# One table for the order of the attention steps in a fused attention and two-MLP kernel

## The chip, the cores and the metric

The kernel runs on one core of a Trainium2 chip. The metric is device time in microseconds (us), the median of three runs. Five engines work side by side, each on its own queue of instructions, strictly in order: TensorE (PE: matrix products; PEld is its weight load), VectorE (DVE), ScalarE (ACT), GpSimd (POOL) and SyncE (SP, which here only issues transfers). Engines wait for each other by semaphores. An instruction that waits holds up everything behind it on its own engine.

## The reference

Causal attention over 2 batches of 12 heads, 448 positions and head width 64, followed by two MLPs on the 896 resulting rows of 768 values (all in float32):

```python
scores = scale * np.matmul(q, k.transpose(0, 1, 3, 2))
scores = np.where(mask, -1000000000.0, scores)      # mask: strictly above the diagonal
scores = scores - np.max(scores, axis=-1, keepdims=True)
attn = np.exp(scores)
attn = attn / (np.sum(attn, axis=-1, keepdims=True) + 1e-09)
x = np.matmul(attn, v)                               # heads side by side: 896 x 768
h = np.maximum(x @ w_in, 0.0);   x = h * h @ w_out   # first MLP, width 2048
h = x @ w_in2;  g = h / (1 + exp(-1.702 h));  out = g @ w_out2
```

## The kernel before

Heads are taken two at a time: a *pair* p (12 in all) is two heads on the two halves of the 128 partitions. Queries are cut in blocks of 128 rows; the scores of a pair come in groups. Group 0 holds query blocks 2 and 0 of both heads (two PSUM banks), group 1 holds block 1 of both heads (two banks), and group 2 the last 64 queries of both heads in one bank. The first pair has group 0 cut in two (groups 3 and 4).

A pair goes through these steps. **Scores** (`scores`, PE). **Minima** (`shifted`, DVE, L266): one instruction per block adds the mask, scales by -1/8, writes the block to SBUF (`pnh`, `pnl`) and returns the row minimum into `stat`; each is followed by a short read of the accumulator. **Exponentials** (`exponentials`, ACT, L283), in place, which also return the row sums. **Sums and reciprocals** (`normalise`, L293 and L294: add 1e-9, then the reciprocal, both on DVE). **Scaling** by the reciprocal (L296, POOL). **Transposes** (`transpose`, PE, L311): 32 blocks into four banks, two banks (one per half) for `g` = 0 and two for `g` = 1. **Copies** out of these banks to `pt` (`keep_transposed`, L316): of each couple of banks one on ACT and one on DVE. **Values** (`values`, PE, L335) into one bank, then the rounded copy (`keep_values`, ACT, L347) and the remainder (`keep_rest`, a subtraction on DVE, L351).

The schedule is written by hand: what stands first in the program stands first in each engine's queue. Ahead of the loop there is a prologue with pairs 0 and 1 up to their exponentials. The loop then makes 12 *turns*; turn p does scores, minima, exponentials and the scaling of group 0 for pair p+2, scaling of the other groups for pair p+1, transposes and copies for pair p, and values for pair p-1. In turns 3 to 8 it also takes pieces of the decoding of the first two weight chunks (64-bit integers into two float parts, `split_w_steps`, on ACT and DVE, L100 to L108), and in turns 10 and 11 pieces of two more. In turns 10 and 11, which have no new scores, PE gets products of the first MLP (`filler`) between the other steps.

PSUM has eight banks from one pool (`ps_p`), and a step that needs a bank waits until the bank's last user has read it. A turn takes ten banks. In the turns between, values (`x`) of a turn take the bank in which the first scores of group 0 of the same turn lay, so they wait for the minima of that head.

Behind the attention the MLPs follow, one product after the other on PE, with weight decoding on DVE and ACT beside them. The change does not touch them.

Of the kernel before, what the change touches and what calls it, by code (L numbers as in the profile page):

```python
# [14 lines left out]
ALU = mybir.AluOpType  # L15
# [3 lines left out]
B, H, S, D = 2, 12, 448, 64  # L19
# [16 lines left out]
WARM = 7  # L36


@with_exitstack
def attention_mlps_kernel(  # L40
# [11 lines left out]
    nc = tc.nc  # L52
# [63 lines left out]
    X = {}  # L116
# [21 lines left out]
    with tc.tile_pool(name="const", bufs=1) as cp, tc.tile_pool(  # L138
# [119 lines left out]
        def shifted(p, g):  # L258
# [4 lines left out]
            work.sort(key=lambda u: u[0])  # L263
# [23 lines left out]
        def normalise(p, gs, eng=nc.gpsimd):  # L287
            if p >= n:
                return
            st = stat[p]  # L290
            work = [u for g in gs for k in range(1 if g == 2 else 2) for u in units(p, g, k)]
            lo, hi = min(u[3] for u in work), max(u[3] for u in work) + 1
            nc.vector.tensor_scalar(st[:, 2, lo:hi], st[:, 1, lo:hi], 1e-9, None, op0=ALU.add)  # L293
            nc.vector.reciprocal(st[:, 2, lo:hi], st[:, 2, lo:hi])  # L294
            for _, _, pn, s, _ in work:
                eng.tensor_scalar(pn, pn, st[:, 2, s : s + 1], 1.0, op0=ALU.mult, op1=ALU.mult)  # L296

        def transpose(p, g):

            if g == 0:  # L300
                PT[p] = qk_p.tile([128, 2, 1024], F32, tag="pt", name="pt")
# [12 lines left out]
        def keep_transposed(p, g):  # L314
            for k, tp in enumerate(tbank.pop((p, g))):
                (nc.vector.tensor_copy if k else nc.scalar.copy)(PT[p][:, k, 512 * g : 512 * g + 512], tp)  # L316
# [38 lines left out]
        for g in (3, 1, 4, 2):  # L355
            scores(0, g)
            shifted(0, g)
            exponentials(0, g)
            if g == 4:
                normalise(0, (3, 1))  # L360
        normalise(0, (4,))
        scores(1, 0)
        scores(1, 1)
        shifted(1, 0)
        normalise(0, (2,), nc.vector)
        exponentials(1, 0)
        scores(1, 2)
        shifted(1, 1)
        exponentials(1, 1)
        shifted(1, 2)  # L370
        exponentials(1, 2)
        normalise(1, (0,))
# [5 lines left out]
        def filler(p):  # L378
            if p + 2 >= n:
                first_term(0, *spare_terms.pop(0), X)  # L380

        def some(k):
            for _ in range(k):
                if decode:
                    decode.pop(0)()

        for p in range(n):
# [9 lines left out]
            many = 2 if p > 9 else 1  # L397
            scores(p + 2, 0)
            scores(p + 2, 1)
            shifted(p + 2, 0)  # L400
            normalise(p + 1, (1, 2))
            exponentials(p + 2, 0)
            filler(p)
            transpose(p, 0)
            transpose(p, 1)
            keep_transposed(p, 0)
            some(many)
            filler(p)
            shifted(p + 2, 1)
            exponentials(p + 2, 1)  # L410
            keep_transposed(p, 1)
            normalise(p + 2, (0,))
            some(many - 1)
            if p > 0:
                values(p - 1)
                keep_values(p - 1)
            filler(p)
            scores(p + 2, 2)
            shifted(p + 2, 2)
            exponentials(p + 2, 2)  # L420
            if p > 0:
                keep_rest(p - 1)
            some(many)
            filler(p)
            some(many - 1)
        first_term(0, 5, 0, X)
        values(n - 1)
        while decode:
            decode.pop(0)()
        keep_values(n - 1)  # L430
        keep_rest(n - 1)
# [144 lines left out]
```

## Time and profile before

| what | us |
|---|---|
| median of 3 runs (551.65 to 560.81) | 551.95 |
| the profiled execution, device time | 551.52 |
| its span in the trace | 549.7 |
| PE busy in the span | 538.6 |
| DVE busy | 354.0 |
| ACT busy | 268.0 |
| POOL busy | 69.3 |

The attention takes about the first 85 us of the span, the MLPs the rest. A view by windows gives the busy time of each engine in a stretch. A timeline gives instructions in order with the idle time of their engine ahead of them in brackets, and what ended it. A start-to-start distance in a timeline is what an instruction costs in a full queue; the duration beside it also holds the instruction's tail, which overlaps with the next one. The granted TensorE clock is 1.00 in every stretch shown.

### The profile page before, as it was taken

What the parts mean: (1) busy time and instruction counts of PE and PEld (TensorE: products, weight loads), DVE (VectorE), ACT (ScalarE), POOL (GpSimd) and SP (SyncE); (2) the same over time, 40 slices, a digit from 0 to 9 for tenths busy, and PEclk for the clock granted to TensorE, in tenths of its full rate; (3) what the DMA queues carried; (4) which work ended last, traced back from release to release, by engine and by line L of the source; (5) the groups of instructions that cost most, each with busy time, mean ns of one, the idle gap of its engine ahead of it and who ended that gap; (6) DMA issues with size and microseconds to landing.
All of it is one profiled execution on the core that took longest, in us unless ns stands there. A gap on an engine that the chain in (4) does not pass through costs nothing.

```text
span 549.7 us, 8778 instructions
## 1 busy us (share of the span) xinstructions
PE 538.6 (98%) x3199; PEld 479.4 (87%) x3199; DVE 354.0 (64%) x806; ACT 268.0 (49%) x610; POOL 69.3 (13%) x115
## 2 busy tenths in 40 slices
PE   8998899999999999999999999999999999999997
PEld 4665678999999999999999999999999999999996
DVE  6988976666666667555465467888878874544420
ACT  6988855666666564233222264555555432222210
POOL 5765630000000000000000011222221100000000
PEclk9999999999999999999999999999999999999999
DMA  7862113343334434333332234334334363443000
GB/s 219 284 188 89 32 30 95 107 116 97 105 115 125 139 129 154 122 109 110 120 86 85 59 87 116 100 103 115 113 109 143 120 199 107 140 148 116 33 35 33
DMA packets 25018, 62.30 MB, mean 113 GB/s; under 512 B 4496, under 2 KB 9744, under 8 KB 24976
## 3 DMA queue, kind: packets, MB, share of 16 engines
q1 hardware_dynamic: 24256, 61.17, 36.6%
q10 hardware_dynamic: 720, 0.57, 0.3%
q8 instruction: 25, 0.41, 0.3%
q14 instruction: 17, 0.14, 0.1%
HBM read 58.98 MB, written 2.75 MB: 112 GB/s over the span
## 4 chain that ended last, share of the span: by engine, by line
PE 89%; ACT 6%; DVE 3%; issue 1%; DVEq 0%; ACTq 0%
PE h L125 14%; PE y L127 14%; PE y L126 14%; PE h L127 14%; PE h L126 14%; PE y L125 14%; ACT pnh L283 4%; DVE pnh L266 2%; PE x L335 1%; ACT pt L316 1%; PE s L238 1%; ACT x L347 1%; PE warm L220 1%; PE s L231 1%; PE t L311 0%
## 5 line engine op out<-in xcount | busy, mean ns | idle before, releaser
L101 ACT CAST wsplit<-m 128x384 fp32r<-128x384 f32 (+1 forms) x112 | 62.7, 560 | 241.5 <-PE y L127 128.4
L125 PE MATMUL h<-x,wsplit 128*128 128x448 f32 x384 | 141.1, 367 | 0.0
L125 PE MATMUL y<-h,wsplit 128*128 128x448 f32 x384 | 140.2, 365 | 0.0
L127 PE MATMUL y<-h,wsplit 128*128 128x448 f32 x384 | 140.2, 365 | 0.0
L126 PE MATMUL y<-h,wsplit 128*128 128x448 f32 x384 | 140.2, 365 | 0.0
L126 PE MATMUL h<-x,wsplit 128*128 128x448 f32 x384 | 140.2, 365 | 0.0
L127 PE MATMUL h<-x,wsplit 128*128 128x448 f32 x384 | 140.2, 365 | 0.0
L102 DVE TENSOR_TENSOR wsplit<-m,wsplit 128x384 fp32r<-128x384 f32 (+1 forms) x112 | 68.8, 614 | 64.1 <-ACT wsplit L101 64.0
L100 DVE CUSTOM_DVE_ANT_0 m<-m,e 128x768 uint16<-128x768 uint16 (+1 forms) x112 | 78.9, 704 | 47.4 <-ACT e L105 34.1
L125 PEld LDWEIGHTS h<-x,wsplit 128*128 128x128 f32 x384 | 72.1, 188 | 6.1 <-DVE stat L293 0.2
L126 PEld LDWEIGHTS h<-x,wsplit 128*128 128x128 f32 x384 | 72.1, 188 | 5.8 <-issue 0.2
L125 PEld LDWEIGHTS y<-h,wsplit 128*128 128x128 f32 x384 | 72.1, 188 | 5.7
L127 PEld LDWEIGHTS y<-h,wsplit 128*128 128x128 f32 x384 | 72.1, 188 | 5.7
L127 PEld LDWEIGHTS h<-x,wsplit 128*128 128x128 f32 x384 | 72.1, 188 | 5.7
L126 PEld LDWEIGHTS y<-h,wsplit 128*128 128x128 f32 x384 | 72.1, 188 | 5.7
L108 DVE SCALAR_TENSOR_TENSOR m<-wraw,m 128x384 uint32<-128x384 uint32 (+1 forms) x112 | 70.3, 628 | 0.0
L105 ACT ACTIVATE e<-wraw 128x384 uint32<-128x384 uint32 (+1 forms) x112 | 67.8, 605 | 0.0
L473 POOL TENSOR_TENSOR h<-g,h 128x448 fp32r<-128x448 f32 x16 | 24.0, 1499 | 336.8 <-ACT h L468 336.8
L106 DVE TENSOR_SCALAR m<-wraw 128x384 uint32<-128x384 uint32 (+1 forms) x112 | 42.6, 380 | 0.0
L283 ACT ACTIVATE pnh<-pnh,stat 128x128 f32<-128x128 f32 (+2 forms) x72 | 35.7, 497 | 7.4 <-DVE stat L266 7.2
L296 POOL TENSOR_SCALAR pnh<-pnh,stat 128x384 f32<-128x384 f32 (+2 forms) x72 | 34.6, 500 | 28.0 <-ACT pnh L283 18.7
L468 ACT CAST h<-g 128x448 fp32r<-128x448 f32 x64 | 34.1, 568 | 3.7 <-DVE g L466 3.5
(54 smaller groups left out, 372.4 us busy)
## 6 DMA issues: line engine op xcount, KB each, us to landing
wraw<-w1i SPq DMA_DIRECT2D x32, 384.0 KB, 3.1
wraw<-w1o SPq DMA_DIRECT2D x24, 512.0 KB, 3.7
wraw<-w2i SPq DMA_DIRECT2D x32, 384.0 KB, 3.1
wraw<-w2o SPq DMA_DIRECT2D x24, 512.0 KB, 3.8
kr<-kT SPq DMA_DIRECT2D x11, 224.0 KB, 3.9
yT<-o SPq DMA_DIRECT2D x11, 224.0 KB, 2.0
v<-v SPq DMA_DIRECT2D x6, 384.0 KB, 3.9
qr<-qT SPq DMA_DIRECT2D x10, 224.0 KB, 4.1
```

The source lines that it names most:

```text
L100: tt(out=m, in0=m, in1=e, op=ALU.add)
L101: nc.scalar.copy(s[:, 0, :], w)
L102: rests.append(lambda: tt(out=s[:, 1, :], in0=w, in1=s[:, 0, :].bitcast(F32), op=ALU.subtract))
L105: lambda: nc.scalar.mul(e, lo, 2.0**-29),
L106: lambda: ts(m, hi, 3, 0x3FFFFFFF, op0=ALU.logical_shift_left, op1=ALU.bitwise_and),
L108: lambda: stt(m, in0=hi, scalar=0xC0000000, in1=m, op0=ALU.bitwise_and, op1=ALU.bitwise_or),
L125: nc.tensor.matmul(ps, ws[:, 0, w], rhs[:, 0, b, :], start=first, stop=False)
L126: nc.tensor.matmul(ps, ws[:, 0, w], rhs[:, 1, b, :], start=False, stop=False)
L127: nc.tensor.matmul(ps, ws[:, 1, w], rhs[:, 0, b, :], start=False, stop=last)
L283: nc.scalar.activation(pn, pn, ACTF.Exp, bias=st[:, 0, s : s + 1], scale=-1.0, accum_out=st[:, 1, s : s + 1])
L296: eng.tensor_scalar(pn, pn, st[:, 2, s : s + 1], 1.0, op0=ALU.mult, op1=ALU.mult)
L468: nc.scalar.copy(h[:, 0, b, :], gs[b])
```

## The change

All steps of the attention are now entries of two tables, `PROLOGUE` and `TURN`: a step's name, and for which pair it is done (in `TURN` a lag relative to the turn). One function `do` runs an entry once per pair. The steps' own arithmetic is as before. These things differ:

- In a turn, PE now does all scores of pair p+2 (groups 0, 2, 1), then both transposes of pair p, then the values of pair p-1. The scores of group 2 were last.
- The minima of groups 1 and 2 and their exponentials move one turn later (lag 1 where it was 2); those of group 0 stay at lag 2, and are last in the turn. On DVE they go head by head (`min0h`).
- The copies out of the transpose banks move one turn later (lag -1), ahead of most other work; three kinds of `kT`: `A` on ACT, `D` on DVE, `M` on ACT for even pairs and on DVE for odd ones. Before, each pair had two on ACT and two on DVE.
- The rounded copy of the values (`xc`) and the remainder (`xr`) move to the turn after the values (lag -2).
- The addition of 1e-9 (`add0`, `add12`) moves from DVE to POOL, except in the prologue; the reciprocals (`rec`) stay on DVE, apart from their sums.
- The prologue computes both pairs' scores of groups 0 and 1 ahead of group 2 and orders minima and exponentials accordingly.
- The first-MLP products in turns 10 and 11 stand together in front of the transposes. Decoding pieces are taken at two places of the turn.

The core of the diff:

```diff
+TURN = (
+    ("kT01A", -1), ("xc", -2), ("some1", 0), ("nrm0", 0), ("kT00M", -1), ("fill", 0), ("min2", 1), ("rec12", 0),
...
+    ("kT10D", -1), ("exp2", 1), ("s0", 2), ("add0", 1), ("xr", -2), ("s2", 2), ("min0h", 2), ("add12", 1),
+    ("s1", 2), ("rec0", 1), ("fill", 0), ("T0", 0), ("T1", 0), ("x", -1), ("exp0", 2),
+)
...
-            work.sort(key=lambda u: u[0])
+            if not by_head:
+                work.sort(key=lambda u: u[0])
...
-            nc.vector.tensor_scalar(st[:, 2, lo:hi], st[:, 1, lo:hi], 1e-9, None, op0=ALU.add)
-            nc.vector.reciprocal(st[:, 2, lo:hi], st[:, 2, lo:hi])
-            for _, _, pn, s, _ in work:
-                eng.tensor_scalar(pn, pn, st[:, 2, s : s + 1], 1.0, op0=ALU.mult, op1=ALU.mult)
...
+        def sums(p, gs, eng):
+            _, at = places(p, gs)
+            eng.tensor_scalar(stat[p][:, 2, at], stat[p][:, 1, at], 1e-9, None, op0=ALU.add)
...
-        def keep_transposed(p, g):
-            for k, tp in enumerate(tbank.pop((p, g))):
-                (nc.vector.tensor_copy if k else nc.scalar.copy)(PT[p][:, k, 512 * g : 512 * g + 512], tp)
+        def keep_transposed(p, g, k, eng):
+            copy = nc.scalar.copy if eng == "A" or (eng == "M" and p % 2 == 0) else nc.vector.tensor_copy
+            copy(PT[p][:, k, 512 * g : 512 * g + 512], tbank[p, g][k])
...
-            scores(p + 2, 0)
-            scores(p + 2, 1)
-            shifted(p + 2, 0)
-            normalise(p + 1, (1, 2))
-            exponentials(p + 2, 0)
-            filler(p)
-            transpose(p, 0)
-            transpose(p, 1)
-            keep_transposed(p, 0)
-            some(many)
-            filler(p)
-            shifted(p + 2, 1)
-            exponentials(p + 2, 1)
-            keep_transposed(p, 1)
-            normalise(p + 2, (0,))
-            some(many - 1)
-            if p > 0:
-                values(p - 1)
-                keep_values(p - 1)
-            filler(p)
-            scores(p + 2, 2)
-            shifted(p + 2, 2)
-            exponentials(p + 2, 2)
-            if p > 0:
-                keep_rest(p - 1)
...
+            for step, lag in TURN:
+                if step == "fill":
+                    filler(p)
+                elif step.startswith("some"):
+                    some(int(step[4:]) * (1 if p < 10 else 3))
+                elif p:
+                    do(step, p + lag)
```

How the queues moved, at three places. First DVE, where the remainder of the values meets the minima of group 0 (`x` is the remainder, `pnh` and `pnl` take the blocks, `t` are transpose banks, a row with `stat` alone reads the accumulator). Before, at the end of turn 1 and the start of turn 2:

```order
L316 COPY pt<-t 128x512
L293 TENSOR_SCALAR stat<-stat 128x4
L294 RECIPROCAL stat<-stat 128x4
L266 ISA pnl_128,stat<-s,last 128x448
L266 ISA stat 128x1
L351 TENSOR_TENSOR x<-x 128x448
L266 ISA pnh_126,stat<-s,mask 128x384
```

The change, in turn 2:

```order
L339 COPY pt<-t 128x512 x2
L374 TENSOR_TENSOR x<-x 128x448
L283 ISA pnh_126,stat<-s,mask 128x384
L283 ISA stat 128x1
L283 ISA pnh_126,stat<-s,mask 128x128
L283 ISA stat 128x1
L283 ISA pnh_126,stat<-s,mask 128x384
```

The remainder still stands right ahead of the minima of group 0, but behind two copies of an older pair; the addition is gone from this queue, and the two blocks of one head now follow each other.

Second ACT, from one rounded copy of the values (`CAST x`) to the next. Before, turns 1 to 2:

```order
L316 COPY pt<-t 128x512
L347 CAST x<-x 128x448
L283 ACTIVATE pnl_128,stat<-pnl_128,stat 128x448
L283 ACTIVATE pnh_126,stat<-pnh_126,stat 128x384 x2
L283 ACTIVATE pnh_126,stat<-pnh_126,stat 128x128 x2
L316 COPY pt<-t 128x512
L283 ACTIVATE pnh_126,stat<-pnh_126,stat 128x256 x2
```

The change, turn 2:

```order
L339 COPY pt<-t 128x512
L370 CAST x<-x 128x448
L300 ACTIVATE pnh_125,stat<-pnh_125,stat 128x256 x2
L300 ACTIVATE pnl_128,stat<-pnl_128,stat 128x448
L300 ACTIVATE pnh_126,stat<-pnh_126,stat 128x384
L300 ACTIVATE pnh_126,stat<-pnh_126,stat 128x128
L300 ACTIVATE pnh_126,stat<-pnh_126,stat 128x384
```

Between the rounded copy and the exponentials of group 0 (`pnh_126`) stood one exponential of 448; now there stand two of 256 more, all of the pair before.

Third PE, one turn. Before (`t` transposes of pair 2, `x` values of pair 1, then scores of group 2 of pair 4 and of groups 0 and 1 of pair 5):

```order
L311 MATMUL t<-ident,pnh_127 128x64 x24
L311 MATMUL t<-ident,pnl_130 128x64 x8
L335 MATMUL x<-pt,v_94 64x384 x2
L335 MATMUL x<-pt,v_94 64x64 x2
L335 MATMUL x<-pt,v_94 64x256 x2
L335 MATMUL x<-pt,v_94 64x64 x2
L335 MATMUL x<-pt,v_94 64x128 x2
L335 MATMUL x<-pt,v_94 64x64 x4
L231 MATMUL s<-kr,ql_86 128x448
L238 MATMUL s<-kr,qr 128x384 x2
L238 MATMUL s<-kr,qr 128x128 x2
L238 MATMUL s<-kr,qr 128x256 x2
```

The change (all scores of pair 4, then the same transposes and values):

```order
L254 MATMUL s<-kr,qr 128x384 x2
L254 MATMUL s<-kr,qr 128x128 x2
L247 MATMUL s<-kr,ql_86 128x448
L254 MATMUL s<-kr,qr 128x256 x2
L334 MATMUL t<-ident,pnh_127 128x64 x24
L334 MATMUL t<-ident,pnl_130 128x64 x8
L358 MATMUL x<-pt,v_94 64x384 x2
L358 MATMUL x<-pt,v_94 64x64 x2
L358 MATMUL x<-pt,v_94 64x256 x2
L358 MATMUL x<-pt,v_94 64x64 x2
L358 MATMUL x<-pt,v_94 64x128 x2
L358 MATMUL x<-pt,v_94 64x64 x4
```

PE does the same matrix work; the scores of group 2 went from behind the values to between the other scores.

## Rows read from the trace of the kernel before

**Rows 1.** The page: span, then PE's busy time, share and instructions.

```profile
span 549.7 us, 8778 instructions
PE 538.6 (98%) x3199; PEld 479.4 (87%) x3199; DVE 354.0 (64%) x806; ACT 268.0 (49%) x610; POOL 69.3 (13%) x115
```

**Rows 2.** Windows: length, busy (instructions) per engine, clock; prologue, turns 2 to 9, rest.

```profile
4.28:14.12 9.84, 8.24 (x73) 5.09 (x72) 8.28 (x44) 8.15 (x31) 4.37 (x10) 1.00 0.80 265
...
20.62:69.39 48.77, 44.30 (x597) 30.26 (x593) 43.50 (x176) 42.95 (x142) 28.41 (x57) 1.00 0.41 127
69.39:90.00 20.61, 20.61 (x208) 16.23 (x205) 13.48 (x30) 10.63 (x25) 3.75 (x8) 1.00 0.21 58
```

**Rows 3.** Windows of single turns: the two without decoding on DVE, the longest of eight.

```profile
20.62:26.40 5.78, 5.44 (x78) 3.73 (x75) 5.06 (x22) 5.21 (x19) 3.45 (x8) 1.00 0.97 308
26.40:32.06 5.66, 5.43 (x78) 3.71 (x74) 5.00 (x22) 5.21 (x18) 3.06 (x8) 1.00 0.61 184
...
56.98:63.38 6.40, 5.44 (x79) 3.72 (x75) 6.13 (x24) 5.24 (x18) 3.99 (x8) 1.00 0.20 63
```

**Rows 4.** Timeline of PE over one turn: start, duration, instruction, [idle before, releaser].

```profile
20.62 1.02 PE L231 MATMUL s<-kr,ql 128*128 128x448 f32 x2
21.57 1.57 PE L238 MATMUL s<-kr,qr 64*128 64x384 f32 x12
22.98 0.92 PE L311 MATMUL t<-ident,pnh 64*128 64x64 f32 x24
...
24.49 1.98 PE L335 MATMUL x<-pt,v 128*64 128x384 f32 x28 [0.34 <-DVE stat L266]
26.40 1.02 PE L231 MATMUL s<-kr,ql 128*128 128x448 f32 x2
```

**Rows 5.** Waits from 14 to 71 us, by engine: total, times, longest.

```profile
PE x L335 <- DVE stat L266: 4.9, 9, 1.0
...
DVE x L351 <- ACT x L347: 2.5, 6, 0.5
...
ACT pnh L283 <- DVE stat L266: 5.8, 8, 1.2
```

**Rows 6.** Timeline of all engines where turn 5 ends and turn 6 begins.

```profile
46.35 0.53 ACT L347 CAST x<-x 128x448 fp32r<-128x448 f32 x1
...
46.91 0.62 DVE L351 TENSOR_TENSOR x<-x 128x448 fp32r<-128x448 f32 x1 [0.47 <-ACT x L347]
...
48.04 0.61 ACT L283 ACTIVATE pnh<-pnh,stat 128x384 f32<-128x384 f32 x1 [0.50 <-DVE stat L266]
...
48.75 1.98 PE L335 MATMUL x<-pt,v 128*64 128x384 f32 x28 [0.39 <-DVE stat L266]
```

**Rows 7.** Timeline: an addition, a reciprocal and a copy on DVE, and what follows.

```profile
48.82 0.17 DVE L293 TENSOR_SCALAR stat<-stat 128x3 f32<-128x3 f32 x1
49.02 0.18 DVE L294 RECIPROCAL stat<-stat 128x3 f32<-128x3 f32 x1
49.11 0.66 DVE L316 COPY pt<-t 128x512 f32<-128x512 f32 x1
49.69 0.41 DVE L266 CUSTOM_DVE_ANT_0 pnh<-s,mask 128x256 f32<-128x256 f32 x1
```

**Rows 8.** Groups of POOL by form: count, total busy us, mean ns, idle before.

```profile
L296 POOL TENSOR_SCALAR pnh<-pnh,stat 128x128 f32<-128x128 f32 x24 | 9.3, 389 | 3.2 <-ACT pnh L283 3.2
...
L565 POOL MEMSET const-float32-0.0<- 128x1 f32 x1 | 0.1, 103 | 0.2 <-issue 0.2
```

**Rows 9.** Timeline: one decoding step on DVE, in turn 7 and in turn 10.

```profile
59.51 0.73 DVE L108 SCALAR_TENSOR_TENSOR m<-wraw,m 128x384 uint32<-128x384 uint32 x1
...
76.02 0.55 DVE L108 SCALAR_TENSOR_TENSOR m<-wraw,m 128x384 uint32<-128x384 uint32 x1
```

**Rows 10.** Timeline: PE and DVE where turn 1 begins.

```profile
14.12 1.02 PE L231 MATMUL s<-kr,ql 128*128 128x448 f32 x2 [0.72 <-DVE stat L266]
...
14.20 0.41 DVE L293 TENSOR_SCALAR stat<-stat 128x3 f32<-128x3 f32 x1
```

More of the change, by code (lines that the diff above doesn't have):

```diff
@@ L36 @@
 WARM = 7
+PROLOGUE = (
[4 rows of a table added]
+)
+TURN = (
[4 rows of a table added]
+)
 @with_exitstack
@@ L256, in units, with shifted @@
             ]
-        def shifted(p, g):
+        def shifted(p, g, by_head):
             if p >= n:
@@ L353, in keep_rest, with do @@
             )
[L355 to L372, printed above, removed]
+        done = set()
+        def do(step, p):
+            if not 0 <= p < n:
+                return
+            name = step.rstrip("ADMh")
+            kind, gs = name.rstrip("0123456789"), [int(g) for g in name if g.isdigit()]
+            if kind in ("add", "rec", "nrm"):
+                if any((kind, p, g) in done for g in gs):
+                    return
+                done.update((kind, p, g) for g in gs)
+            elif (name, p) in done:
+                return
+            done.add((name, p))
+            on_vector = step.endswith("D")
+            if kind == "s":
+                scores(p, gs[0])
+            elif kind == "min":
+                shifted(p, gs[0], step.endswith("h"))
+            elif kind == "exp":
+                exponentials(p, gs[0])
+            elif kind == "add":
+                sums(p, gs, nc.vector if on_vector else nc.gpsimd)
+            elif kind == "rec":
+                reciprocals(p, gs)
+            elif kind == "nrm":
+                normalise(p, gs, nc.vector if on_vector else nc.gpsimd)
+            elif kind == "T":
+                transpose(p, gs[0])
+            elif kind == "kT":
+                keep_transposed(p, *gs, step[-1])
+            else:
+                {"x": values, "xc": keep_values, "xr": keep_rest}[kind](p)
+        for step, p in PROLOGUE:
+            do(step, p)
         load_qk(3)
@@ L378, in filler @@
         def filler(p):
-            if p + 2 >= n:
+            if p + 2 >= n and spare_terms:
                 first_term(0, *spare_terms.pop(0), X)
@@ L396, in attention_mlps_kernel @@
                 decode += split_w_steps(len(wsplit)) + [lambda i=len(wsplit) + 3: load_w(i)]
[L397 to L427 removed]
+            for step, lag in TURN:
[5 more added lines that the diff above has]
+                    do(step, p + lag)
+                else:
+                    for q in range(lag + 1):
+                        if q or step.startswith(("T", "kT", "x")):
+                            do(step, q)
+        for p in (n, n + 1):
+            for step, lag in TURN:
+                if p + lag < n and not step.startswith(("some", "fill")):
+                    if p + lag == n - 1 and step == "x":
+                        while spare_terms:
+                            first_term(0, *spare_terms.pop(0), X)
+                        first_term(0, 5, 0, X)
+                    do(step, p + lag)
         while decode:
             decode.pop(0)()
[L430 to L431 removed]
     hp_ = ctx.enter_context(tc.tile_pool(name="hp_", bufs=KF))
```

15 lines of the change are left out of this document (9 added, 6 removed), and 5 rows, old and new, of tables (PROLOGUE, TURN).

## The prediction

> **What bounds the kernel now.** I read the page first: PE is busy 538.6 of 549.7 us [rows 1], so no order of the other engines can give back more than the 11.1 us in which PE stands idle, and that is 2.0% of the time. I then cut the span by windows [rows 2]. From 69.39 us on PE has no gap that matters (20.61 of 20.61 up to 90 us); the MLPs behind it are one product after another. What can be won lies in front: a prologue to 14.12, then turns 1 to 9. I count a turn from one score matmul of group 2 to the next: turn 1 begins at 14.12 [rows 10], turn 9 ends at 69.39, nine turns in 55.3 us, 6.14 each. The eight from 20.62 on take 48.77 us, 6.10 each.
>
> What does such a turn need? PE's timeline over turn 2 [rows 4] runs from 20.62 to 26.40, 5.78, with 0.34 of idle time: 5.44 us of work that no order removes. DVE is busy 43.50 us in the eight turns, 5.44 each, but unevenly [rows 2, 3]: 5.03 in the two turns without decoding, so (43.50 - 10.06) / 6 = 5.57 in the others. ACT has 42.95 / 8 = 5.37, POOL 28.41 / 8 = 3.55. Three engines thus need about 5.4 and the turn takes 6.1: the missing 0.7 are waits in a ring. The sums of waits name it [rows 5]: PE's values wait for DVE's minima (4.9 us, 9 times), ACT's exponentials for DVE's minima (5.8, 8 times), DVE's remainder for ACT's copy (2.5, 6 times). Rows 6 show it once, in order: ACT rounds the values at 46.35; DVE waits 0.47 for that and subtracts at 46.91; only then come the minima of group 0, for which ACT has waited 0.50 when it starts at 48.04, and PE 0.39 when its values start at 48.75, since they need the bank of the first head.
>
> **The ring, term by term.** In the new order DVE's remainder still stands ahead of the minima, but the rounded copy is asked of ACT at the head of the turn, while DVE's subtraction stands behind the minima of groups 2 and 1 and two copies, so that wait goes. ACT's exponentials of group 0 stand last in ACT's turn, behind 1.6 us or more of exponentials of the pair before, so that they need the minima later. PE does all scores first; the values come behind the scores that they share a bank with by 0.95 for group 2 (20.62 to 21.57 [rows 4]), some 0.5 of the 1.41 for groups 0 and 1, and 1.17 for the transposes (22.98 to 24.49 less the idle 0.34): 2.6 us, in which the minima of the second head have to come. The remainder and the minima of both heads take 1.91 together (46.91 to 48.82 [rows 6, 7]). So each of the three waits has cover. What is late next is whichever engine has most work.
>
> **Work that changes engine.** Two additions per turn leave DVE: 0.20 from an addition to the next instruction [rows 7], 0.40 in all. Half a copy per turn comes to DVE from ACT: a copy costs 0.58 there [rows 7], so 0.29. DVE has 5.03 - 0.40 + 0.29 = 4.92 without decoding and 5.57 - 0.11 = 5.46 with it. ACT loses about as much as DVE gets, an estimate, 5.37 - 0.29 = 5.08. POOL gets two tiny additions, which no row shows there. Below, a one-column memset took 0.10; above, a 128x128 scaling 0.39 [rows 8]. I take 0.3, nearer the scaling because it is the same operation. POOL then has 3.55 + 0.6 = 4.15, at most 4.33, with over a microsecond free.
>
> The change also adds waits. Both reciprocals on DVE now wait for POOL. Behind the one of group 0, DVE's last step of a turn, stand the next turn's minima of groups 2 and 1, and PE's next scores want their banks. POOL runs scaling of group 0, then of groups 1 and 2, then the two additions; from one reciprocal to the addition that the next one needs it has 3.55 + 0.3 = 3.9 us of work in a turn of 5.4, so I cost this at nothing; without that cover it would cost the overhang. On ACT the rounded copy, now second in the turn, waits for the end of PE's values, with a copy and all exponentials behind it; 5.08 us of work in a 5.44 turn leave 0.36 for that, and less in turns that also hold a decoding step and the extra copy.
>
> **Sum for the turns.** The floor is max(5.44, 4.92) = 5.44 without decoding and max(5.44, 5.46) = 5.46 with it: nine turns in 49.1. The ceiling I set by the two turns of before that have no decoding, 5.78 and 5.66 [rows 3], which still hold the ring. Engines that are 92 to 100% full and wait for each other in strict order don't reach the floor; I take 5.6, the middle: 50.4, which is 4.9 less than 55.3.
>
> **The prologue.** DVE is full there (8.28 of 9.84 busy [rows 2]), and its work stays, except that the additions for groups 1 and 2 of pair 1 and group 0 of pair 2 go to POOL: 0.44 for the one at 14.20, which waited, with its reciprocal next at 14.64 [rows 10], and 0.20 for the other. The copies of pair 0 go behind the first scores' minima into turn 1. PE's wait of 0.72 ahead of the scores of group 2 [rows 10] goes, but the second transpose bank now wants a minimum of pair 2. Bounds 0 and 0.9; I take 0.5.
>
> **The end of the attention, and the MLPs.** Behind turn 9 PE has the same transposes, values and nine products left, and had no gap [rows 2]. The new order puts four products (12 matmuls) in front of each transpose, time for the scaling and copies of the pair; I cost it at nothing. If that cover is short, PE idles there, up to about 1 us. The transfers on SP stand in the same order as before, and keep the 16 DMA engines 41% busy over the turns, so starting 5 us sooner finds them ready. Clock: granted 1.00 in every stretch before; PE gets only denser.
>
> Sum: 4.9 + 0.5 = 5.4. The profiled execution took 551.52, which gives 546.1. The median of the runs shown is 551.95, 0.43 more; on that scale I predict **546.5 us**.
>
> **A rule that speaks against it.** Row first: a decoding step on DVE took 0.73 in turn 7, beside a busy POOL, and 0.55 in turn 10 without [rows 9]. The Trainium skill, "GPSIMD Engine Reference", section 1 (Specifications), says that GpSimd shares its SBUF interfaces with VectorE and that they contend when a VectorE instruction has two SBUF inputs or runs in a two-port mode. This trace agrees with it.
>
> **Rivals.**
> - *DVE and POOL collide.* Two-input steps stretch by 0.73 / 0.55 = 1.33. Decoding is (5.57 - 5.03) x 6 = 3.2 us on DVE; POOL now works at the head of each DVE turn, where these pieces stand. If all of it stretched once more: 3.2 x 0.33 = 1.1, all on the bound: 547.6. For it: rows 9. Against: some of the decoding is stretched already in the 3.2, and minima, copies and remainders read PSUM.
> - *The ring moves instead of opening.* ACT runs late, so its rounded copy, DVE's remainder, the minima behind it and PE's values are late in turn. For it: ACT has only 0.36 to spare. Then turns stay at 5.9 to 6.1: saved 0.4 to 2.2, with the prologue 549.3 to 551.1.
> - *Slower: POOL becomes the loop.* The reciprocal of group 0 waits for POOL's addition, the next scaling for the reciprocal. That loop is 3.55 + a plus two handovers of about 0.1, so 3.75 + a with a the price of one addition. It decides from a = 1.7 on (turn 5.44), passes the time of before at a = 2.4 (turn 6.14), and slows the kernel by 2% (11 us over nine turns, turn 7.4) at a = 3.6. Against: that is nine times the dearest near row, 0.39. A turn of 6.5 would give 551.95 + 9 x 0.36 - 0.5 = 554.7.
> - *Better than forecast.* Floor turns and the full 0.9: 6.2 + 0.9 = 7.1, so 544.8. More than 2% would need nearly all of PE's 11.1 us, including the wait for the first transfers at the start.
>
> **How the numbers follow.** Forecast (turns of 5.45 to 5.85, with the prologue between its bounds 544.8 to 549.3): 0.68. Collision as the deciding effect: 0.10. Ring moved: 0.15. Loop through POOL: 0.04. Better than 544.5: 0.03. The range from 544.3 to 550.2 holds the forecast, the collision and the better half of the moved ring. Two per cent either way, about what a measurement of this kernel tells from no change, is 540.9 and 563.0: faster 0.02, within 0.94, slower 0.04.
>
> **What the profile after would show.** Turns of about 5.6 between score matmuls of group 2; waits of DVE's remainder for ACT near zero; values waiting less than 0.2 a turn for minima; DVE busy about 5.0 and 5.5 a turn; POOL's additions at 0.1 to 0.4 and no reciprocal waiting for them; PE reaching the first MLP product about 5.4 sooner and nothing changed behind. The prediction is wrong if reciprocals wait for POOL, if ACT's rounded copy waits and the minima with it, or if PE idles in turns 10 and 11.

## The result and the profile after

The changed kernel takes 546.27 us (median of 4 runs, 545.8 to 546.54); the kernel before, run beside it, takes 551.65. Several kernels, the one before among them, had single executions some 9 us longer, and the medians given from here on leave those out. The ratio is 0.990, with a 95% interval from 0.989 to 0.992: 5.4 us or about 1% less, within two per cent, 0.2 us from the forecast of 546.5 and inside its range. The profiled execution took 546.54 us, against 551.52 of before.

The page comes first: the span, PE's busy time with that of the other engines, and the shares of the chain that ended last.

```profile
span 544.6 us, 8744 instructions
PE 539.2 (99%) x3199; PEld 480.6 (88%) x3199; DVE 353.3 (65%) x791; ACT 265.7 (49%) x604; POOL 75.7 (14%) x136
PE 98%; DVE 1%; issue 0%; ACT 0%; ACTq 0%
```

Against [rows 1] the span is 5.1 us shorter, and PE's busy time is 0.6 us longer. Idle time of PE was 549.7 - 538.6 = 11.1 and is 544.6 - 539.2 = 5.4. In the kernel before, the chain that ended last had 89% on PE, 6% on ACT and 3% on DVE; now it is PE nearly throughout.

The windows answer to [rows 2] and [rows 3]. A turn is counted from one first score matmul to the next (group 0 now; group 2 before). The rows are the prologue, turn 1, turns 2 to 9 together, the first of them, and the rest to 90 us. Columns: window, length, then busy time (instructions) of PE, PEld, DVE, ACT, POOL, the granted clock, the DMA share and GB/s.

```profile
4.28:14.44 10.16, 9.38 (x75) 5.85 (x75) 8.75 (x46) 8.46 (x32) 5.56 (x12) 1.00 0.79 264
14.44:20.53 6.09, 6.09 (x75) 4.17 (x74) 6.09 (x27) 6.09 (x23) 4.00 (x11) 1.00 0.95 281
20.53:65.27 44.74, 44.74 (x596) 31.14 (x593) 42.75 (x166) 40.76 (x137) 32.40 (x73) 1.00 0.46 139
...
65.27:90.00 24.73, 24.73 (x231) 20.80 (x228) 16.56 (x34) 12.36 (x28) 6.32 (x12) 1.00 0.24 65
```

Turn 9 now ends at 65.27. In turns 2 to 9 the profile shows no idle time on PE: 44.74 of 44.74 us, where it had 44.30 of 48.77 in eight turns of before. The mean turn is 44.74 / 8 = 5.59; six of the eight are 5.56, turns 4 and 6 are 5.70 and 5.68, and turn 1, ahead of them, is 6.09. Behind, PE is still without a gap. The two kernels' turns don't start at the same matmul, so for a like count I take the start of the first scores of group 0 in turn 1 in both: 15.07 before, 14.44 after. From there to the same place nine turns later (before: 69.39 and 0.95 of group 2) it was 70.34 - 15.07 = 55.27 and is 65.27 - 14.44 = 50.83. So the turns gave 4.4 us and the prologue 0.6.

PE's busy time is modelled, and in the three longer turns it hides a wait for a PSUM bank. The scores of group 0 take 1.07 from their start to the next scores in the six short turns, but 1.22 in turn 4, 1.18 in turn 6 and 1.61 in turn 1. Turn 4 begins like this:

```profile
31.18 0.57 ACT L339 COPY pt<-t 128x512 f32<-128x512 f32 x1
31.65 1.29 PE L254 MATMUL s<-kr,qr 64*128 64x384 f32 x8
32.87 1.02 PE L247 MATMUL s<-kr,ql 128*128 128x448 f32 x2
```

ACT's copy out of a transpose bank ends at 31.18 + 0.57 = 31.75, and the second head's scores, which take that bank, load their first weights at 31.81. In turn 6 it is the same (copy until 42.41 + 0.57 = 42.98, weights at 43.03). In turn 1 the second head's weights, at 14.98, wait for a minimum on DVE. The three waits come to 0.8 us.

The waits from 13 to 66 us answer to [rows 5] (engine, tile, line, what it waited for: total, times, longest):

```profile
ACT x L370 <- PE x L358: 3.7, 6, 0.9
...
DVE x L374 <- ACT x L370: 1.1, 2, 0.8
...
PE t L334 <- DVE stat L283: 0.8, 1, 0.8
...
ACT pnh L300 <- POOL stat L311: 0.4, 1, 0.4
```

Two of the three waits of the ring are gone: PE's values no longer wait for minima (4.9 us before), nor ACT's exponentials (5.8 before). The remainder's wait for ACT fell from 2.5 to 1.1. The only wait of a PE matmul that the view lists is a single one of a transpose, 0.8, ahead of turn 1. In their place stands ACT's rounded copy, which waits for the end of PE's values; nothing late follows from it, as this timeline of all engines at the head of turn 5 shows. It answers to [rows 6] (start, duration, engine, line, instruction, [idle before, releaser]).

```profile
37.47 0.54 ACT L370 CAST x<-x 128x448 fp32r<-128x448 f32 x1 [0.62 <-PE x L358]
...
38.06 0.61 DVE L374 TENSOR_TENSOR x<-x 128x448 fp32r<-128x448 f32 x1
...
38.59 0.54 DVE L283 CUSTOM_DVE_ANT_0 pnh<-s,mask 128x384 f32<-128x384 f32 x1
38.79 0.52 ACT L300 ACTIVATE pnh<-pnh,stat 128x256 f32<-128x256 f32 x1
...
39.79 0.66 ACT L300 ACTIVATE pnl<-pnl,stat 128x448 f32<-128x448 f32 x1
...
40.44 0.61 ACT L300 ACTIVATE pnh<-pnh,stat 128x384 f32<-128x384 f32 x1
```

The rounded copy runs right behind the values. Then come the remainder and the first minima of group 0 on DVE, at 38.06 and 38.59. While DVE makes these, ACT is busy with the exponentials of groups 1 and 2 of the pair before, and those of group 0 then start at 40.44 with nothing to wait for.

### The profile page after: what moved, and what is told of

Read it like the earlier page. It is cut to its first block, busy times and chain, and to the rows that moved or that the text cites. A ratio compares the mean times of both kernels' runs of the same rounds, so it can differ in the third digit from the quotient of the medians.

```text
span 544.6 us, 8744 instructions
## 1 busy us (share of the span) xinstructions
PE 539.2 (99%) x3199; PEld 480.6 (88%) x3199; DVE 353.3 (65%) x791; ACT 265.7 (49%) x604; POOL 75.7 (14%) x136
## 4 chain that ended last, share of the span: by engine, by line
PE 98%; DVE 1%; issue 0%; ACT 0%; ACTq 0%
PE h L141 14%; PE h L143 14%; PE y L143 14%; PE y L141 14%; PE y L142 14%; PE h L142 14%; PE x L358 4%; PE s L254 3%; PE t L334 2%; PE s L247 2%; DVE pnh L283 1%; PE warm L236 1%; DVE pnl L283 0%; DVE pnl L319 0%; DVE stat L315 0%
## 5 line engine op out<-in xcount | busy, mean ns | idle before, releaser
L124 DVE SCALAR_TENSOR_TENSOR m<-wraw,m 128x384 uint32<-128x384 uint32 (+1 forms) x112 | 70.3, 628 | 0.0
L122 DVE TENSOR_SCALAR m<-wraw 128x384 uint32<-128x384 uint32 (+1 forms) x112 | 43.1, 384 | 0.0
L319 POOL TENSOR_SCALAR pnh<-pnh,stat 128x384 f32<-128x384 f32 (+2 forms) x72 | 35.7, 516 | 7.8 <-DVE stat L315 5.2
L300 ACT ACTIVATE pnh<-pnh,stat 128x384 f32<-128x384 f32 (+2 forms) x72 | 35.8, 502 | 1.9 <-DVE stat L283 1.5
```

The costliest lines, as they stand in the source:

```text
L122: lambda: ts(m, hi, 3, 0x3FFFFFFF, op0=ALU.logical_shift_left, op1=ALU.bitwise_and),
L124: lambda: stt(m, in0=hi, scalar=0xC0000000, in1=m, op0=ALU.bitwise_and, op1=ALU.bitwise_or),
L300: nc.scalar.activation(pn, pn, ACTF.Exp, bias=st[:, 0, s : s + 1], scale=-1.0, accum_out=st[:, 1, s : s + 1])
L319: eng.tensor_scalar(pn, pn, stat[p][:, 2, s : s + 1], 1.0, op0=ALU.mult, op1=ALU.mult)
```

## The experiments

The theory: the gain comes from where the rounded copy `xc` stands in ACT's queue, ahead of some 1.6 us of other exponentials, so that the remainder and the minima behind it are done when ACT and PE ask for them. The rivals: the additions on POOL, which take 0.4 us a turn off DVE; the lag of the copies; the prologue; PE's order of scores.

**1. The one move undone: the rounded copy behind the other exponentials.** Everything else is as in the changed kernel.

```diff
-    ("kT01A", -1), ("xc", -2), ("some1", 0), ("nrm0", 0), ("kT00M", -1), ("fill", 0), ("min2", 1), ("rec12", 0),
+    ("kT01A", -1), ("some1", 0), ("nrm0", 0), ("kT00M", -1), ("fill", 0), ("min2", 1), ("rec12", 0),
...
-    ("kT10D", -1), ("exp2", 1), ("s0", 2), ("add0", 1), ("xr", -2), ("s2", 2), ("min0h", 2), ("add12", 1),
+    ("kT10D", -1), ("exp2", 1), ("xc", -2), ("s0", 2), ("add0", 1), ("xr", -2), ("s2", 2), ("min0h", 2), ("add12", 1),
```

> The changed kernel with one entry moved: ACT's rounded copy of the values stands behind the exponentials of groups 1 and 2, right ahead of those of group 0, as it did before the change (there with one exponential between). Theory (the ring runs from the rounded copy over DVE's remainder and minima to ACT's exponentials of group 0, and it was opened by the 1.6 us of exponentials that now stand behind the rounded copy): ACT must idle from the copy's end to the first minimum, 0.1 + 0.54 + 0.48 + 0.1 = 1.2 a turn, and its loop becomes 1.97 + 0.47 + 0.24 + 0.3 + 0.99 + 0.65 + 0.43 + 1.2 = 6.25 instead of 5.56: nine turns cost 5 to 6 us, 551 to 552.5, all of the gain. Rival (the gain lies in the order of the scores on PE, the lag of the copies or the load of DVE): 546.3, no change.

Measured: 553.37 us, ratio to the kernel before 1.003 [1.002, 1.004]. That is 7.1 us more than the changed kernel: the whole gain and more. Its waits from 14 to 71 us:

```profile
ACT pnh L300 <- DVE stat L283: 9.8, 8, 1.3
DVE x L374 <- ACT x L370: 8.6, 7, 1.8
...
PE t L334 <- DVE stat L283: 2.7, 7, 0.4
```

And its timeline where the ring closes:

```profile
33.99 0.65 ACT L300 ACTIVATE pnl<-pnl,stat 128x448 f32<-128x448 f32 x1
...
34.64 0.51 ACT L370 CAST x<-x 128x448 fp32r<-128x448 f32 x1
35.18 0.62 DVE L374 TENSOR_TENSOR x<-x 128x448 fp32r<-128x448 f32 x1
...
35.72 0.55 DVE L283 CUSTOM_DVE_ANT_0 pnh<-s,mask 128x384 f32<-128x384 f32 x1
...
36.37 0.62 ACT L300 ACTIVATE pnh<-pnh,stat 128x384 f32<-128x384 f32 x1 [1.23 <-DVE stat L283]
```

Now all other exponentials come first, the rounded copy after them, and ACT has nothing left to do while DVE makes remainder and minima: it idles 1.23 ahead of the exponentials of group 0, at about the 1.2 expected. The ring is back, longer than in the kernel before. The mechanism held, and so did its price: the nine turns take 56.81 us (14.27 to 71.08) instead of 50.83, 6.0 more where 5 to 6 were expected. I had not counted what follows: in turns 10 and 11 another 1.1 us goes, with a transpose that waits 0.52 for POOL's scaling at 80.28.

**2. The one move alone, in the kernel before.** The rounded copy, with the values ahead of it, goes ahead of group 1's exponentials.

```diff
             transpose(p, 1)
+            if p > 0:
+                values(p - 1)
             keep_transposed(p, 0)
             some(many)
+            if p > 0:
+                keep_values(p - 1)
             filler(p)
...
             some(many - 1)
-            if p > 0:
-                values(p - 1)
-                keep_values(p - 1)
```

> The kernel before with one step moved: ACT's rounded copy of the values of pair p-1 goes ahead of the exponentials of groups 1 and 2 of its turn (the values' matmuls keep their place on PE in turns 1 to 9; in turns 10 and 11 they come ahead of one first-MLP product). Nothing else of the change: additions on DVE, old order of scores, copies and minima, old prologue. Theory (the place of that copy on ACT is the cause): the waits of DVE's remainder for ACT and of ACT's exponentials for the minima go, turns fall from 6.10 to 5.5 to 5.7, 547.0 to 548.5. Rival (several parts are needed together, a PSUM bank keeps the ring closed): 551 to 552. The additions and the prologue would then be worth the rest.

Measured: 548.07 us, ratio 0.993 [0.991, 0.996], as expected. This one move brings 3.6 of the 5.4 us. Window over its turns 2 to 9, and below it the waits from 14 to 71 us that are left of [rows 5]:

```profile
20.70:66.00 45.30, 43.45 (x596) 29.74 (x592) 42.72 (x176) 42.91 (x141) 29.05 (x57) 1.00 0.47 141
```

```profile
PE x L335 <- DVE stat L266: 2.2, 5, 0.5
ACT pnh L283 <- DVE stat L266: 1.6, 4, 0.5
```

Turns are 45.30 / 8 = 5.66, those without a stall 5.44 to 5.45, which is PE's own work. The values' wait fell from 4.9 to 2.2, the exponentials' from 5.8 to 1.6; the remainder's wait for ACT doesn't occur any more.

**3. Additions: back on DVE in the changed kernel.**

```diff
-    ("kT10D", -1), ("exp2", 1), ("s0", 2), ("add0", 1), ("xr", -2), ("s2", 2), ("min0h", 2), ("add12", 1),
+    ("kT10D", -1), ("exp2", 1), ("s0", 2), ("add0D", 1), ("xr", -2), ("s2", 2), ("min0h", 2), ("add12D", 1),
```

> The changed kernel with the additions of 1e-9 given back to DVE (all else as changed). In the changed kernel turns 2 to 9 take 5.59 us each with PE never idle, while DVE is busy 42.75 / 8 = 5.34. Theory (the ring of waits was cut, PE is the bound, DVE is next): DVE gets 0.40 a turn, 5.74 on average, so turns go to about 5.75, 1.5 us in all: 547.8. Rival (taking the additions off DVE is what carries the gain): nine turns lose 0.40 each, 3.6 us, 549.9 or more. Rival (DVE has spare time in every turn): 546.3, no change.

Measured: 546.42 us, ratio 0.991 [0.989, 0.993], which can't be told from the changed kernel; six of turns 2 to 9 are still 5.56, turns 4 and 6 5.69 and 5.66. The theory missed, the second rival (spare time on DVE) held. Window over turns 2 to 9:

```profile
20.42:65.13 44.71, 44.71 (x596) 31.08 (x592) 44.37 (x180) 40.83 (x137) 28.49 (x57) 1.00 0.47 145
```

DVE is busy 44.37 of 44.71 us, and PE still shows no gap. DVE's work just fits under PE's.

**4. Additions: on POOL in the kernel before, and on POOL beside the move of the rounded copy.** The first is the diff below; the second is it and the diff of experiment 2 together.

```diff
-        def normalise(p, gs, eng=nc.gpsimd):
+        def normalise(p, gs, eng=nc.gpsimd, adds=nc.vector):
...
-            nc.vector.tensor_scalar(st[:, 2, lo:hi], st[:, 1, lo:hi], 1e-9, None, op0=ALU.add)
+            adds.tensor_scalar(st[:, 2, lo:hi], st[:, 1, lo:hi], 1e-9, None, op0=ALU.add)
...
-            normalise(p + 1, (1, 2))
+            normalise(p + 1, (1, 2), adds=nc.gpsimd)
...
-            normalise(p + 2, (0,))
+            normalise(p + 2, (0,), adds=nc.gpsimd)
```

> The kernel before with one part of the change alone: in the turns the additions of 1e-9 go from DVE to POOL. Theory (DVE's additions are not in the ring: it runs over the remainder, the first minimum, and ACT): 551.2 to 551.8, hardly any change. Rival (the load of DVE bounds the turns of before): 0.40 a turn over nine turns, 548.1.

> The kernel before with ACT's rounded copy early (548.1 by itself) and also the additions of the turns on POOL (552.4 by itself, no gain). In the first of these, values still wait for minima 2.2 us in five turns, those with decoding on DVE. Theory (with the ring open DVE's load counts in those turns): 0.40 less on DVE takes most of these waits, 546.5 to 547.3. Rival (the remaining waits come from a decoding step between the remainder and the minima, which the additions don't touch, or reciprocals wait for POOL): 548.1 or up to 1 us more.

Measured: 552.36 (ratio 1.001 [1.000, 1.002]) and 548.55 (0.994 [0.993, 0.996], beside 0.993 for the move alone). No gain in either. The waits of the first one, from 14 to 71 us, show why the 0.4 us that leave DVE don't arrive:

```profile
ACT pnh L283 <- DVE stat L266: 5.4, 8, 1.0
PE x L335 <- DVE stat L266: 4.5, 9, 0.7
...
DVE x L351 <- ACT x L347: 3.6, 8, 0.7
...
DVE stat L294 <- POOL stat L293: 1.4, 2, 1.0
...
ACT pnh L283 <- POOL stat L293: 1.0, 1, 1.0
```

Two of the ring's waits are hardly shorter than in [rows 5], and the third, of DVE's remainder for ACT's copy, grew from 2.5 to 3.6: part of the time that DVE gained it now waits there. Two new waits on POOL stand beside them: 1.4 for reciprocals, 1.0 for exponentials. So the additions on POOL carry none of the change's gain. My expectation for the second kernel, that the decoding turns would profit, fell.

**5. Copies back in their own turn.** The four `kT` steps leave their lag of -1.

```diff
-    ("kT01A", -1), ("xc", -2), ("some1", 0), ("nrm0", 0), ("kT00M", -1), ("fill", 0), ("min2", 1), ("rec12", 0),
+    ("xc", -2), ("some1", 0), ("nrm0", 0), ("fill", 0), ("min2", 1), ("rec12", 0),
...
     ("s1", 2), ("rec0", 1), ("fill", 0), ("T0", 0), ("T1", 0), ("x", -1), ("exp0", 2),
+    ("kT01A", 0), ("kT00M", 0), ("kT11D", 0), ("kT10D", 0),
```

> The changed kernel with the four copies out of the transpose banks taken back into the turn of their transposes (lag 0, behind the exponentials of group 0); all else as changed. Theory (the lag of the copies is part of what opens the ring): DVE's copies then wait for PE's transposes and stand between them and the next minima of groups 2 and 1, which PE's next scores wait for: 0.1 + 1.16 (or 1.75 in every second turn) + 0.55 + 0.1 + 0.35 behind the transposes, against 1.91 of values on PE, so 0.4 to 1.0 of idle PE per turn, 6.2 to 6.3 a turn, 551 to 552.5. Rival (only the lag of the remainder matters): 546.3, no change.

Measured: 547.9 us, ratio 0.993 [0.992, 0.995]: 1.6 more than the changed kernel, a third of what was expected. DVE's copies wait for transposes (`DVE pt` for `PE t`: 2.8 us, 5 times), but while they do, PE has the values of the pair before to compute, 1.91 us of work. Most turns are 5.56; PE is 0.46 later at the end of turn 1, turns 7, 8 and 9 take 5.71, 5.69 and 6.04, and 0.65 goes behind the last.

**6. The old order of the prologue.** `PROLOGUE` in the order that the kernel before runs, turns unchanged.

```diff
-    ("s3", 0), ("min3", 0), ("s1", 0), ("s4", 0), ("min1", 0), ("min4", 0), ("exp3", 0), ("exp1", 0), ("s0", 1),
+    ("s3", 0), ("min3", 0), ("exp3", 0), ("s1", 0), ("min1", 0), ("exp1", 0), ("s4", 0), ("min4", 0), ("exp4", 0),
...
```

> The changed kernel with the prologue's steps in the old order (the turns as changed). Theory: the prologue is bound by DVE, whose work is the same, and the scores of turn 1 start at 14.44 instead of 15.07, so it is worth about 0.6: 546.9. Rival (the new prologue also sets the turns in phase, so that more hangs on it): 547.5 to 549. Rival (worth nothing, given back in turn 1, which takes 6.09): 546.3.

Measured: 546.63 us, ratio 0.991 [0.989, 0.993]: 0.36 more, near what was expected, though the intervals overlap. The scores of turn 1 start at 14.47, hardly later than 14.44 in the changed kernel; PE's first values come at 18.90 instead of 18.62.

**7. Three small parts undone together.** Additions on DVE, minima of group 0 by block, copies always two on ACT and two on DVE.

```diff
-    ("kT01A", -1), ("xc", -2), ("some1", 0), ("nrm0", 0), ("kT00M", -1), ("fill", 0), ("min2", 1), ("rec12", 0),
+    ("kT01A", -1), ("xc", -2), ("some1", 0), ("nrm0", 0), ("kT00A", -1), ("fill", 0), ("min2", 1), ("rec12", 0),
...
-    ("kT10D", -1), ("exp2", 1), ("s0", 2), ("add0", 1), ("xr", -2), ("s2", 2), ("min0h", 2), ("add12", 1),
+    ("kT10D", -1), ("exp2", 1), ("s0", 2), ("add0D", 1), ("xr", -2), ("s2", 2), ("min0", 2), ("add12D", 1),
```

> The changed kernel with three parts undone together: additions back on DVE, minima of group 0 block by block instead of head by head, copies two on ACT and two on DVE for every pair. DVE gets 0.40 - 0.29 a turn, ACT 0.24 or more. Theory (none of the three carries the gain; the place of the rounded copy on ACT does): 546.3 to 547.3. Rival (together they hold the turns open, since ACT's and DVE's spare time is only some 0.3 a turn): 548 to 550.

Measured: 546.93 us, ratio 0.992 [0.990, 0.994]: about 0.7 more, and the intervals overlap. By these medians the three together are worth about an eighth of the gain.

**8. The remainder early too.** A control on the other side: `xr` follows `xc` at the head of DVE's turn, ahead of copies and minima of groups 1 and 2.

```diff
-    ("kT01A", -1), ("xc", -2), ("some1", 0), ("nrm0", 0), ("kT00M", -1), ("fill", 0), ("min2", 1), ("rec12", 0),
+    ("kT01A", -1), ("xc", -2), ("xr", -2), ("some1", 0), ("nrm0", 0), ("kT00M", -1), ("fill", 0), ("min2", 1), ("rec12", 0),
...
-    ("kT10D", -1), ("exp2", 1), ("s0", 2), ("add0", 1), ("xr", -2), ("s2", 2), ("min0h", 2), ("add12", 1),
+    ("kT10D", -1), ("exp2", 1), ("s0", 2), ("add0", 1), ("s2", 2), ("min0h", 2), ("add12", 1),
```

> The changed kernel with one entry moved: DVE's remainder of the values stands at the head of its turn, ahead of the minima of groups 2 and 1, instead of behind the copies. Theory (what stands between the rounded copy and the remainder on DVE is the cover of that wait): DVE waits at its head for the end of PE's values and ACT's copy, 0.1 + 0.43 + 0.1, and the minima that PE's next scores want come 0.54 + 0.55 + 0.1 + 0.35 later; PE idles some 2 us a turn, 558 to 564. Rival (DVE reaches that place late anyway): 546.3 to 548.

Measured: 569.62 us, 23 more than the changed kernel and beyond what was expected (558 to 564). Its DVE timeline at the head of a turn:

```profile
36.07 0.62 DVE L374 TENSOR_TENSOR x<-x 128x448 fp32r<-128x448 f32 x1 [2.56 <-ACT x L370]
36.61 0.68 DVE L339 COPY pt<-t 128x512 f32<-128x512 f32 x1
```

DVE stands 2.56 us still, and all that it does behind the remainder is late. PE waits for it three times over: the second head's next scores for the bank that the remainder reads (PE `s` for DVE `x`, 14 to 85 us: 2.6, 6 times), and the transposes for minima (2.6, 7 times) and copies (0.6, 3 times). The remainder in turn needs the values of the turn before, rounded by ACT. So from one pair's values to the next one's a chain now runs through ACT's rounding, the remainder and what is queued behind it on DVE. I had counted the late minima but not the bank and the copies, and values start 7.4 to 8.2 us apart.

**9. Could PE's own work be shorter?** Three orders of the scores. (a) Groups 0, 1, 2; (b) 0, 1, 2 with the changed kernel's order of bank use; (c) 2, 0, 1 with the banks of group 0 taken first. The step `bank` in (b) and (c) only allocates.

```diff
-    ("kT10D", -1), ("exp2", 1), ("s0", 2), ("add0", 1), ("xr", -2), ("s2", 2), ("min0h", 2), ("add12", 1),
+a   ("kT10D", -1), ("exp2", 1), ("s0", 2), ("s1", 2), ("add0", 1), ("xr", -2), ("s2", 2), ("min0h", 2), ("add12", 1),
+b   ("kT10D", -1), ("exp2", 1), ("s0", 2), ("add0", 1), ("xr", -2), ("bank", 2), ("min0h", 2), ("add12", 1),
+c   ("kT10D", -1), ("exp2", 1), ("bank", 2), ("s2", 2), ("s0", 2), ("add0", 1), ("xr", -2), ("min0h", 2), ("add12", 1),
...
-    ("s1", 2), ("rec0", 1), ("fill", 0), ("T0", 0), ("T1", 0), ("x", -1), ("exp0", 2),
+a   ("rec0", 1), ("fill", 0), ("T0", 0), ("T1", 0), ("x", -1), ("exp0", 2),
+b   ("s1", 2), ("s2", 2), ("rec0", 1), ("fill", 0), ("T0", 0), ("T1", 0), ("x", -1), ("exp0", 2),
+c   ("s1", 2), ("rec0", 1), ("fill", 0), ("T0", 0), ("T1", 0), ("x", -1), ("exp0", 2),
```

> The changed kernel with PE's scores in the order of groups 0, 1, 2 instead of 0, 2, 1 (minima and all else as changed). In the changed kernel the scores of groups 0 and 1 take 1.07 + 0.53 = 1.60 a turn, before the change 1.41, where they stood together; PE changes twice more between matmuls on half the rows and on all rows. Theory (the split costs PE 0.15 a turn, and PE is the bound): turns of 5.41 to 5.45, 1.0 to 1.3 us less, 545.0 to 545.3. Rival (the difference is only how rows are grouped in the trace, or DVE binds at once, since the first scores now wait for a later minimum): 546.3 or up to 1 us more.

> The changed kernel with PE's scores in the order of groups 0, 1, 2, but with the banks taken in the changed kernel's order (0, 2, 1), in the turns and in turn 0. In the order 2, 0, 1 the scores of groups 0 and 1 took 1.40 a turn instead of 1.60, but the transposes 1.29 instead of 1.10, as the minima of group 0 came later; in the order 0, 1, 2 with its own banks they took 1.50 and 1.14. Theory (scores kept together cost PE 1.40; what was lost again were bank waits): turns of 1.40 + 0.95 + 1.10 + 1.91 = 5.36 to 5.45, DVE next at 5.46 in turns with decoding, 0.9 to 1.5 us less than the changed kernel: 544.8 to 545.4. Rival (PE needs 5.5 in every order that has the group 2 scores next to halves): 546.0 to 546.5.

> The changed kernel with PE's scores in the order of groups 2, 0, 1; the banks of group 0 are still taken first, so that every step waits for the same kind of bank. The sequence on PE then changes only twice a turn between matmuls that use all 128 rows and those that use halves (values and group 2 | groups 0 and 1 and transposes), as before the change; the changed kernel and the order 0, 1, 2 change four times. Theory (the changes cost PE its longer turns: 5.56 and 5.51 against 5.44 of work before): turns of 5.44 to 5.48, 0.7 to 1.1 us less than the changed kernel, 545.2 to 545.6. Rival (DVE binds at 5.46 in turns with decoding and the first scores now wait for a later minimum): 546.0 to 547.0.

Measured: (a) 546.46, ratio 0.990 [0.989, 0.992]; (b) 545.97, 0.990 [0.988, 0.992]; (c) 545.76, 0.989 [0.988, 0.991]. None can be told from the changed kernel, and all three theories missed. Turns are 5.50 to 5.52 in (a), but its first one starts 0.42 later, and 5.50 to 5.52 in (b); in both, turns 4 and 6 are longer (5.71 and 5.66; 5.75 and 5.67). In (c) they are 5.55, turn 4 5.62. PE's timeline over the turn head in the changed kernel, then in (b), then in (c):

```profile
26.09 1.14 PE L254 MATMUL s<-kr,qr 64*128 64x384 f32 x8
27.16 1.02 PE L247 MATMUL s<-kr,ql 128*128 128x448 f32 x2
28.11 0.70 PE L254 MATMUL s<-kr,qr 64*128 64x256 f32 x4
28.64 0.91 PE L334 MATMUL t<-ident,pnh 64*128 64x64 f32 x24
29.38 0.43 PE L334 MATMUL t<-ident,pnl 64*128 64x64 f32 x8
29.74 1.98 PE L358 MATMUL x<-pt,v 128*64 128x384 f32 x28
```

```profile
25.76 1.57 PE L254 MATMUL s<-kr,qr 64*128 64x384 f32 x12
27.26 1.02 PE L247 MATMUL s<-kr,ql 128*128 128x448 f32 x2
28.21 0.96 PE L334 MATMUL t<-ident,pnh 64*128 64x64 f32 x24
```

```profile
26.20 1.02 PE L247 MATMUL s<-kr,ql 128*128 128x448 f32 x2
27.15 1.57 PE L255 MATMUL s<-kr,qr 64*128 64x384 f32 x12
28.55 1.06 PE L335 MATMUL t<-ident,pnh 64*128 64x64 f32 x24
29.39 0.47 PE L335 MATMUL t<-ident,pnl 64*128 64x64 f32 x8
29.84 0.54 PE L359 MATMUL x<-pt,v 128*64 128x384 f32 x2
```

Read start to start. With group 2 between groups 0 and 1 the scores of both cost 1.07 + 0.53 = 1.60; in one run of twelve they cost 1.50 in (b) and 1.40 in (c). In (c) the gain is lost again at the transposes, 29.84 - 28.55 = 1.29 instead of 1.10, since the minima of group 0 start later there (DVE waits 2.1 us for these scores, 4 times).

## Why the prediction was right, step by step

- **The ring** was the right bound and the right gain. Experiments 1 and 2 show it from both sides: undone alone it costs 7.1 us, done alone in the old kernel it brings 3.6. Of the three covers, that of ACT was the one that decided; the values' wait needed more, since in experiment 2 it is still there in five turns.
- **The turns**: 5.6 forecast, 5.59 measured for eight, 5.65 with the first. The saving was 4.4 where I said 4.9. The number was near, but its reason held only in part. I put 0.16 over the floor of 5.44 because full engines that wait for each other don't reach it. In six of the nine turns nothing of this kind shows: they take 5.56, whether DVE is busy 4.80 or 5.56 us of them, and what lies over the floor is PE's own time. For the scores of groups 0 and 1 in one run [rows 4] give 1.41; I took this over although the diff itself splits them. That was the mis-sized term: 1.60, 0.19 a turn, of which 0.07 comes back at the transposes (1.10 instead of 1.17). In these turns the waits between the other engines cost nothing. Turns 1, 4 and 6 do lose 0.8 us to waits. Those of turns 4 and 6 are for ACT, which was busy 5.44 us in the turn before, each with a decoding step and the extra copy: the case that I had named and not priced.
- **Work that changes engine**: DVE 42.75 / 8 = 5.34 a turn (4.92 and 5.46 forecast, 5.33 in the mean), ACT 40.76 / 8 = 5.10 (5.08), POOL 32.40 / 8 = 4.05 (4.15). The sizes held, but this part was worth nothing: experiments 3 and 4. With PE as the bound DVE may be 99% full (experiment 3). An addition on POOL costs 0.25 and 0.24, between the bounds of 0.10 and 0.39. POOL's groups by form (count, total, mean ns, idle before):

```profile
L311 POOL TENSOR_SCALAR stat<-stat 128x3 f32<-128x3 f32 x11 | 2.8, 251 | 12.7 <-ACT pnl L300 11.1 <-DVE stat L315 1.5
L311 POOL TENSOR_SCALAR stat<-stat 128x4 f32<-128x4 f32 x10 | 2.4, 242 | 0.8
```

- **The prologue**: 0.5 forecast, and scores of group 0 0.63 earlier. The size was right; its reasons are not shown. With the old order put back these scores start at 14.47 (experiment 6), with the additions back on DVE at 14.25 (experiment 3), against 14.44: neither of the two brought the 0.63. It comes with something else of the change ahead of turn 1, and no run took that apart. PE's wait for a minimum at the second transpose bank, which I had set against the gain, is there: 0.79 at 13.75.
- **The end**: cost at nothing, and PE has no gap there (24.73 of 24.73). The values of the last pair start at 77.53 where they started at 82.70, 5.2 earlier, and the span is 5.1 shorter. Nothing was given back in the MLPs.
- **The sum**: 4.4 + 0.6 = 5.0 on the profiled executions (4.98 between their times), 5.4 forecast. Two terms were off by 0.5 and 0.1 in opposite directions. That the median came within 0.2 us of the forecast is in part luck: the profiled execution after is the slowest of its four, and I had scaled the forecast up by 0.43 to a median of three runs, 551.95, where the kernel before took 551.65 beside the change.
- **The rivals.** Ring moved: not as a ring. The wait that was to start it is there, ACT's rounded copy for the values, 3.7 us in all, and twice the remainder was late with it (by 0.29 in turn 3 and 0.77 in turn 9), but both turns took 5.56: the 1.6 us of exponentials behind the copy still cover DVE. ACT's lateness shows only in the 0.3 us of turns 4 and 6. POOL as the loop: not seen, no reciprocal waits for an addition. Collision of DVE and POOL: there, but hidden under PE. Decoding steps on DVE in turns 2, 9 and 10 of the changed kernel, and a scaling on POOL beside the last:

```profile
24.60 0.70 DVE L122 TENSOR_SCALAR m<-wraw 128x384 uint32<-128x384 uint32 x1
...
65.00 0.77 DVE L124 SCALAR_TENSOR_TENSOR m<-wraw,m 128x384 uint32<-128x384 uint32 x1
...
68.88 0.32 DVE L122 TENSOR_SCALAR m<-wraw 128x384 uint32<-128x384 uint32 x1
...
69.86 1.02 POOL L319 TENSOR_SCALAR pnh<-pnh,stat 128x384 f32<-128x384 f32 x1
69.89 0.53 DVE L124 SCALAR_TENSOR_TENSOR m<-wraw,m 128x384 uint32<-128x384 uint32 x1
```

The steps at 24.60 and 65.00 ran while POOL was busy throughout, the one at 68.88 while it did nothing. At 69.89 both were at work too, but there DVE took its short time, and POOL's scaling 1.02 where such a scaling takes 0.63 on average. The step L124 at 47.87 is such a case too: 0.56, beside a POOL that was busy throughout. So a busy POOL doesn't by itself make DVE's step long; whether the loss falls on DVE, on POOL or on both, no run here took apart. The Trainium skill, "GPSIMD Engine Reference", section 1 (Specifications), tells of contention over shared SBUF interfaces between GpSimd and VectorE instructions with two SBUF inputs or in a two-port mode. The rows of L124, which has two inputs, agree with it; L122 has one tensor as input, and no row shows its mode. The rival failed because DVE was no longer the bound: none of the three hidden waits of PE is for a decoding step.

**What stays open.** The move of the rounded copy accounts for 3.6 of the 5.4. The rest, 1.8, wasn't taken apart one by one: the order of the prologue's steps is about 0.4 of it, the copies' lag is worth 1.6 inside the changed kernel, and the three small parts together about 0.7; these overlap. The later minima and exponentials of groups 1 and 2 were not moved back alone. Why the same scores take 1.50 behind the values and 1.40 behind group 2's stays open too. It is hardly a wait for a bank: ahead of the first 64-row weight load behind group 2's scores the profile shows the same 0.65 of idle time in each of turns 1 to 9, before and after the change, and names another releaser from turn to turn.

## What to carry to other kernels

When engines are each 90% full and still wait, follow one ring of waits and look, on each engine in it, for work that doesn't belong to the ring: the step that starts the ring goes ahead of that work, the step that ends it behind. Here that one place in one queue was worth more than any work moved between engines. And when a change reorders matmuls, take PE's own time from rows in the new order or widen the term, since a floor read from the old order need not be one.

## What the runs showed of the hardware

- Scores by 64 rows cost 1.40 to 1.60 us for the same twelve matmuls, by what stands before and between them.
- A 128x3 addition on POOL takes 0.25 us against 0.39 for a 128x128 scaling [rows 8]: with 3 or 4 columns (0.25 and 0.24) nearly all of it is a fixed price.
- A decoding step with one tensor as input (L122) took 0.70 (24.60) and 0.53 (42.50) beside a busy POOL and 0.32 (68.88) without; in the kernel before, one took 0.37 (72.88) beside a busy POOL. The two-input step took 0.77 or 0.53 to 0.56 beside a busy POOL and 0.55 without. I had reckoned with the two-input steps only.
- A PE that the profile shows busy without a gap can still be waiting: in turn 1 it was busy 6.09 of 6.09 us, 0.54 of them a wait of the second head's scores for a bank.
